# Attention's row maxima subtracted by TensorE, one exp for a step, and other places for loads and tiles

## The chip, the cores and the metric

One core of a Trainium2 chip runs the whole program in one launch. The metric is device time in microseconds (us). The engines are TensorE (PE, with its weight loads as PEld), VectorE (DVE), ScalarE (ACT), GpSimd (POOL) and SyncE (SP), which here only issues transfers.

## The reference, cut to what matters

```python
scores = scale * np.matmul(q, k.transpose(0, 1, 3, 2))        # (4, 8, 576, 64) inputs
...
scores = np.where(masks[None, :, :, :], scores, -1000000000.0)
scores = scores - np.max(scores, axis=-1, keepdims=True)
attn = np.exp(scores)
attn = attn / (np.sum(attn, axis=-1, keepdims=True) + 1e-09)
return np.matmul(attn, v).astype(np.float32)
```

Four heads see a plain window of 32 keys, four a dilated one (32 keys, 4 apart). The result, 2304 tokens by 512, goes through two mixtures of 8 experts. In the first, each token goes to one expert (288 tokens an expert) by a greedy assignment. In the second, every expert sees every token, and the outputs are weighed by a matrix P that 8 rounds of row and column scaling balance.

## The kernel before

**Attention.** The work is cut into 24 blocks (4 batches by 6 blocks of 96 queries), each against 128 keys. A unit holds kind 0 (plain) of one block and kind 1 (dilated) of the block after it, so there are 25 units (`NU`); the first and the last hold one kind alone. The loop over `n` (L303) gives the engines this order, and each engine works through its own instructions in it:

- `scores(n)`: PE writes the masks into two PSUM banks, as a bf16 identity (`idb`) times the mask table (L169), and adds q times k for eight heads (L176, f32, 64 rows each, so that two heads share the array).
- `row_max(n)`: DVE takes the maximum of each row and head (L182), and ACT turns it into a bias (L183).
- `p_trans(n-1)` on PE (L200), then `p_evac` of it, a copy of 768 columns from PSUM by DVE (L207).
- `exps(n)`: ACT, one instruction for each of the eight heads, the maximum as its bias (L192).
- `x_out(n-3)`: halves of the finished rows by ACT and POOL, stores by SP.
- `pv(n-2)`: PE multiplies by v (L218) and, in some iterations, adds the router's logits (L288) and turns finished rows (L258); DVE divides by the sums.

`scores` has two PSUM slots, `p_trans` and `pv` have one each. Beside this, `side` loads and splits the first weights of the second mixture (L742 on ACT, L744 on DVE). SP issues the loads: for the first batch, kind 1 of k and q with all 576 columns, then kind 0 of both, then v. ACT's queue issues the masks and an f32 identity, from which DVE makes `idb` (L293).

**Stage 1** (the router and the first mixture) ends with `m2_l1(8)` and `m2_l2(8)`. The first of these reads the tiles `x2` (L848, names x2h and x2l); the second reads the weights in the pool `m_w` (L936, names w1h and w1l). The balancing of P (`sinkhorn`, L1233) is placed between their matmuls by a planner (`interleave`).

**Stage 2** is the second mixture: seven experts over three blocks of 384 tokens, with products by a seven-multiplication scheme. `x_load` (L1048) brings a block's input into the tile `xb` with two transfers; `s_l1` (L1120) reads it. Pools opened in stage 2 lie one behind the other in the memory that stage 1 gave up: first `n_t` (29,184 bytes a partition by its tiles), then `n_x` with `xb` (21,504), then `n_h`. Stage 1's pools in that memory were, from low addresses to high, `m_x2` (36,864 bytes), then `m_w`.

Of the kernel before, what the change touches and what calls it, by code (L numbers as in the profile page):

```python
# [11 lines left out]
F32 = mybir.dt.float32  # L12
F16 = mybir.dt.float16
BF = mybir.dt.bfloat16
I32 = mybir.dt.int32
AF = mybir.ActivationFunctionType
OP = mybir.AluOpType
AX = mybir.AxisListType

B, H, S, D = 4, 8, 576, 64  # L20
# [3 lines left out]
QB = 96  # L24
# [7 lines left out]
SC = 0.125  # L32
# [26 lines left out]
MASK_ID, MASKS = attention_masks()  # L59
# [22 lines left out]
NU = len(UNITS)  # L82
# [29 lines left out]
def attention(tc, q, k, v, masks, wg, ident, xd, L, zero, side, early, keep, tables):  # L112

    nc = tc.nc
    with ExitStack() as ctx:
# [5 lines left out]

        raw, T, VR, SS, PP, PT, XT = {}, {}, {}, {}, {}, {}, {}
        src = {"q": q, "k": k}
        def load_qk(nm, b, kind):
            x = raw[nm, b, kind] = ld.tile([128, 2, S], F32, name="raw%s%d" % (nm, kind))
            nc.sync.dma_start(x, src[nm][b, :, 2 * kind:2 * kind + 2])

        def load_v(b, kind):
            x = VR[b, kind] = vp.tile([128, NJ, 4, D + 1], F32, name="rawv%d" % kind, bufs=2)
            nc.sync.dma_start(x, v[b, kind])  # L130

        def part(u, size):

            ks = list(UNITS[u])
            return slice(ks[0] * size // 2, (ks[-1] + 1) * size // 2)

        idf = one.tile([128, 128], F32)
        idb = one.tile([QB, QB], BF)
        idh = one.tile([QB, QB], F16)
        mk = one.tile([QB, MASKS.shape[1], 2, 128], BF)  # L140
        wgf = one.tile([128, 4, E], F32)
        wgh = one.tile([128, 4, E], F16)
        wgl = one.tile([128, 4, E], F16)
        for kind in (1, 0):
            for nm in "kq":
                load_qk(nm, 0, kind)
            if kind:
                nc.scalar.dma_start(mk, masks)
                nc.scalar.dma_start(idf, ident)
        load_v(0, 1)  # L150
        load_v(0, 0)

        def warm(n):
# [25 lines left out]
        def row_max(u):  # L179
            p, gs = SS[u], part(u, 4)  # L180
            nm = wk.tile([QB, 2, 4], F32, name="nm")
            nc.vector.tensor_reduce(nm[:, :, gs], p[:, :, gs], axis=AX.X, op=OP.max)  # L182
            nc.scalar.activation(nm[:, :, gs], nm[:, :, gs], AF.Copy, scale=-SC)  # L183
            PP[u] = nm

        def exps(u):
            p, nm, gs = SS.pop(u), PP[u], part(u, 4)
            e = wk.tile([QB, 2, 4, 128], F32, name="e")
            PP[u] = e
            for s in range(2):  # L190
                for g in range(gs.start, gs.stop):
                    nc.scalar.activation(e[:, s, g, :], p[:, s, g, :], AF.Exp, bias=nm[:, s, g:g + 1], scale=SC)  # L192
                yield

        def p_trans(u):
            e, gs = PP.pop(u), part(u, 4)
# [6 lines left out]
        def p_evac(u, p):  # L203
            gs = part(u, 4)
            t = PT[u] = wk.tile([128, 2, 4, QB], F32, name="pt")
            pp = p[:, :, :4 * QB].rearrange("p s (g q) -> p s g q", g=4)
            nc.vector.tensor_copy(t[:, :, gs], pp[:, :, gs])  # L207

        def pv(u, extra, turn=None):
            t = PT.pop(u)  # L210
# [79 lines left out]
            return lambda: nc.vector.tensor_copy(L[:, c, :], p)  # L290

        warm(18)
        nc.vector.tensor_copy(idb, idf[:QB, :QB])  # L293
        nc.vector.tensor_copy(idh, idf[:QB, :QB])
        loaded = []
        for kind in (1, 0):
            for nm in "kq":
# [2 lines left out]
            load_v(1, kind)  # L300
        xl = [one.tile([128, 2, 2, S], F16, name="xl%d" % kind) for kind in range(2)]
        first = S * (B - 1) // 128
        for n in range(NU + 2):  # L303
            if n < NU:
                scores(n)
                row_max(n)
            if 1 <= n <= NU:
                p_evac(n - 1, p_trans(n - 1))
            ex = exps(n) if n < NU else iter(())
            next(ex, None)  # L310
            if 3 <= n <= NU:
                x_out(n - 3)
            for _ in ex:
                pass
            if n == NU:
                early()
            if n in FILL:
                warm(FILL[n])
            if n >= 2:
                pv(n - 2, [loaded.pop(0)[1] for _ in range(1 if n < NU else 3) if loaded and loaded[0][0] <= n],  # L320
                   n - 3 if NU - 4 <= n <= NU else None)
            if n == 1:
                nc.gpsimd.dma_start(wgf, wg)
                tables()
            elif n == 4:
                nc.scalar.activation(wgh, wgf, AF.Copy, scale=SG)
                nc.vector.scalar_tensor_tensor(wgl, wgf, SG, wgh, op0=OP.mult, op1=OP.subtract)
            if 4 <= n:
                next(side, None)
            if n == 9:  # L330
                tables(True)
            b, c = divmod(n - NJ - 2, NJ)
            if 0 <= b < B - 2 and c < 2:
                load_v(b + 2, 1 - c)
            b, c = divmod(n - NJ, NJ)
            if 0 <= b < B - 2 and c < 2:
                for nm in "kq":
                    load_qk(nm, b + 2, 1 - c)
            b, c = divmod(n - 10, NJ)
            if 0 <= b < B - 1 and c < 3:  # L340
                c0, c1 = S * b // 128, S * (b + 1) // 128
                c0, c1 = c0 + 2 * c, min(c0 + 2 * c + 2, c1)
                if c1 > c0:
                    x_load(c0, c1)
                    loaded += [(n + 3, i) for i in range(c0, c1)]
            if n == NU - 1:
                x_load(first, first + 1)
            if n == NU:
                loaded += [(n, i) for i in (first, first + 1)]
# [36 lines left out]
THR = step_constants()  # L386
# [32 lines left out]
class Router:  # L419
# [35 lines left out]
    def tables(self, made):  # L455
        nc, col = self.nc, self.col
        tab, thr = self.source
        if not made:
            nc.gpsimd.dma_start(self.t, tab)
            nc.gpsimd.dma_start(self.thr, bass.AP(tensor=thr.tensor, offset=thr.offset, ap=[[0, 128], [1, THR.size]]))  # L460
            return
        nc.gpsimd.tensor_copy(self.tri, col("tri"))
        nc.gpsimd.tensor_copy(self.val, col("val").rearrange("p (c v) -> p c v", v=2))
        nc.gpsimd.tensor_copy(self.iota, col("iota"))
        nc.gpsimd.tensor_copy(self.diag, col("diag")[:E])
        nc.gpsimd.tensor_copy(self.group, col("group"))
# [200 lines left out]
class Moe:  # L667
# [34 lines left out]
    def tables(self, made):  # L702
        if made:
            self.nc.gpsimd.tensor_copy(self.id16, self.idf)
        else:
            self.nc.gpsimd.dma_start(self.idf, self.ident)

    def kept(self, ctx):
        self.xp = ctx.enter_context(self.tc.tile_pool(name="m_x", bufs=1, side="right"))
# [40 lines left out]
    def psum(self):  # L750
        return self.ps.tile([128, 512], F32, name="mm", bufs=6)

    def warm(self, n):

        p = self.psum()
        for _ in range(n):
            self.nc.tensor.matmul(p, self.zero[:, :128], self.zero, start=True, stop=True)

    def weights(self, key, fetch):

# [608 lines left out]
    def stage2(self, ctx):  # L1369


        pool = lambda n, b: ctx.enter_context(self.tc.tile_pool(name=n, bufs=b))
        self.tp, self.bp, self.hp = pool("n_t", 1), pool("n_x", 1), pool("n_h", 1)

        def part():
            lo = self.tp.tile([128, 2, 2, BLK], F32, name="r", bufs=2).bitcast(F16).rearrange(
                "p a b m -> p (a b m)")[:, :7 * 256].rearrange("p (k c) -> p k c", k=7)
            return self.tp.tile([128, 3, BLK], F32, name="S", bufs=1)[:, :, :256], lo

        def l1(e, n, b):  # L1380
            for j, ns in enumerate(self.s_l1(b)):
                if n and e + 1 < E and j in (0, 1, 3):
                    next(new)
                yield ns

        self.x_load(0)
        for _ in range(6):
            self.warm(1)
        for e in range(1, E):
            order = list(range(NB))[::1 if e % 2 else -1]  # L1390
            new = self.staged(e + 1, part) if e + 1 < E else iter(())
            for n, b in enumerate(order):
                if n == 0:
                    next(new, None)
                interleave(l1(e, n, b), self.side if (e, n) == (1, 0) else None)
                if n + 1 < NB:
                    self.x_load(order[n + 1])
                elif e + 1 < E:
                    self.last_piece()
                    self.w_load(0)  # L1400
                for j, _ in enumerate(self.s_l2(e)):
                    if j in (8, 10, 16, 20, 23, 43):
                        next(new, None)
                if n + 1 == NB:
                    for _ in new:
                        pass
                    if e + 1 < E:
                        self.w_load(1)
# [27 lines left out]


def constants():
    return dict(masks=MASKS.astype(ml_dtypes.bfloat16), ident=np.eye(128, dtype=np.float32), rtab=RTAB, thr=THR)


# [12 lines left out]
```

## Time and profile before

| what | value |
|---|---|
| time, median of 3 runs | 1805.51 us (1804.84 to 1808.44) |
| time of the profiled execution | 1803.2 us |
| its span, first to last instruction | 1801.4 us |
| PE busy | 1738.0 us (96%) |
| DVE busy | 1359.0 us (75%) |
| ACT busy | 852.7 us (47%) |
| mean granted TensorE clock | 0.982 |

A matmul's row in the trace begins when it begins to stream and ends when its last result is modelled to be written. Matmuls overlap, so what one costs in a row of many is the distance between starts, not its length. The granted clock is a share of 2.4 GHz. "x16" is a merged row of 16 instructions. The name behind an arrow in square brackets is what ended an idle time.

### The profile page before, as it was taken

Reading aid. Unit: us, or ns where it says so; the run is one execution under the profiler, and the core shown is the slowest. Engines: PE = TensorE matmul, PEld = TensorE weight load, DVE = VectorE, ACT = ScalarE, POOL = GpSimd, SP = SyncE. Lnnn points to the kernel's source line nnn. Section 1 sums busy time; section 2 is a strip of 40 time slices with the busy share of each in tenths; the row PEclk is TensorE's granted clock in tenths of the full one; section 3 lists DMA queues with packets and bytes.
Section 4 is the critical chain, followed back from the end, with each engine's and each line's share of the span. In section 5 each row is a group of like instructions: output and inputs, shape, how many; then the busy total and the mean of one; then the engine's idle time right before and its main releaser. Section 6 shows DMA issues by size and latency. Waiting matters only on the chain.

```text
span 1801.4 us, 35276 instructions
## 1 busy us (share of the span) xinstructions
PE 1738.0 (96%) x14464; PEld 1290.0 (72%) x14464; DVE 1359.0 (75%) x2583; ACT 852.7 (47%) x1581; POOL 239.6 (13%) x297
## 2 busy tenths in 40 slices
PE   9986899999999989999999999999999999999998
PEld 7864676667776657777777777777777777777776
DVE  6977785678744858878887888788788878887556
ACT  5853442343443345555554456444455544464433
POOL 2423331223320000000000000000000000000111
PEclk9977999999999999999999999999999999999999
DMA  8923441424442132445225443424452254433020
GB/s 295 288 65 108 121 121 61 131 78 121 143 139 67 57 130 98 170 154 201 114 89 206 159 150 133 162 101 170 157 197 116 90 202 159 150 134 154 36 97 36
DMA packets 105554, 241.20 MB, mean 134 GB/s; under 512 B 46192, under 2 KB 69888, under 8 KB 98480
## 3 DMA queue, kind: packets, MB, share of 16 engines
q1 hardware_dynamic: 84592, 151.27, 24.3%
q0 software_dynamic: 20544, 87.42, 13.8%
q8 instruction: 113, 1.85, 0.4%
q14 instruction: 49, 0.40, 0.1%
q10 hardware_dynamic: 256, 0.26, 0.0%
HBM read 173.63 MB, written 61.73 MB: 131 GB/s over the span
## 4 chain that ended last, share of the span: by engine, by line
PE 72%; DVE 11%; issue 10%; ACT 4%; DMA 2%; POOL 1%; SPq 0%; POOLq 0%; ACTq 0%; DVEq 0%
PE mm L1120 27%; PE mm L1158 23%; PE mm L848 8%; PE mm L936 5%; PE mm L892 2%; PE r L542 1%; PE ps_v L218 1%; DVE hl L1077 1%; PE ps_p L200 1%; PE ps_s L176 1%; POOL out_dram L1172 1%; DVE G L488 1%; DVE w1l L789 1%; DVE G L615 1%; ACT w1h L788 1%
## 5 line engine op out<-in xcount | busy, mean ns | idle before, releaser
L1120 PE MATMUL mm<-xb,w1h 128*128 128x384 f16 x2352 | 574.8, 327 | 7.8 <-issue 4.8
L1158 PE MATMUL mm<-w2h,hh 128*128 128x256 f16 x1764 | 480.8, 273 | 0.4
L1158 PE MATMUL mm<-w2h,hl 128*128 128x256 f16 x1764 | 480.8, 273 | 0.0
L1158 PE MATMUL mm<-w2l,hh 128*128 128x256 f16 x1764 | 480.8, 273 | 0.0
L1120 PE MATMUL mm<-xb,w1l 128*128 128x384 f16 x1176 | 383.9, 326 | 0.0
L1158 PEld LDWEIGHTS <-hh 128*128 128x128 f16 x3528 | 345.2, 98 | 43.1 <-issue 0.9
L1120 PEld LDWEIGHTS <-w1h 128*128 128x128 f16 x2352 | 230.3, 98 | 159.5 <-issue 11.4
L1158 PEld LDWEIGHTS <-hl 128*128 128x128 f16 x1764 | 172.6, 98 | 19.9
L1077 DVE TENSOR_TENSOR hl<-r,hh 128x1536 f16<-128x1536 f32 x84 | 147.5, 1756 | 42.7 <-ACT hh L1076 42.7
L1120 PEld LDWEIGHTS <-w1l 128*128 128x128 f16 x1176 | 115.2, 98 | 79.3 <-issue 3.5
L1072 ACT ACTIVATE r<-mm 128x384 f32<-128x384 f32 x252 | 119.1, 481 | 100.0 <-PE mm L1120 100.0
L1038 POOL DMA_DIRECT2D ws<-raw x48 | 26.1, 543 | 944.1 <-ACT raw L989 532.3
L1076 ACT ACTIVATE hh<-r 128x1536 f16<-128x1536 f32 x84 | 124.6, 1483 | 43.6 <-DVE r L1101 41.6
L1083 ACT ACTIVATE mm<-mm 128x384 f32<-128x384 f32 x84 | 40.3, 479 | 185.0 <-PE mm L1120 185.0
L1077 DVE TENSOR_TENSOR hl<-S,hh 128x1152 f16<-128x1152 f32 x84 | 113.6, 1352 | 0.0
L1168 DVE SCALAR_TENSOR_TENSOR acc<-t,P,acc 128x512 f32<-128x512 f32 x126 | 94.7, 752 | 4.5
L848 PE MATMUL mm<-xt,w1h 128*128 128x288 f16 x512 | 95.9, 286 | 1.7 <-DVE xt L865 1.7
L1076 ACT ACTIVATE hh<-S 128x1152 f16<-128x1152 f32 x84 | 96.3, 1147 | 0.0
L854 DVE SCALAR_TENSOR_TENSOR w1l<-mm,w1h 128x288 f16<-128x288 f32 (+1 forms) x120 | 50.3, 437 | 60.4 <-ACT w1h L853 59.8
L989 ACT ACTIVATE raw<-raw 128x1024 f16<-128x1024 f32 x48 | 50.6, 1055 | 87.3 <-DVE raw L973 45.5
L853 ACT ACTIVATE w1h<-mm 128x288 f16<-128x288 f32 (+1 forms) x120 | 46.9, 395 | 80.9 <-PE mm L848 78.4
L848 PE MATMUL mm<-x2l,w0h 128*128 128x256 f16 x288 | 79.9, 278 | 3.8 <-DVE x2l L897 3.8
(271 smaller groups left out, 2973.4 us busy)
## 6 DMA issues: line engine op xcount, KB each, us to landing
xb<-xw SPq DMA_DIRECT2D x30, 1344.0 KB, 8.7
ws<-raw POOLq DMA_DIRECT2D x48, 448.0 KB, 3.9
ws<-r POOLq DMA_DIRECT2D x48, 448.0 KB, 3.1
raw<-in_w2b_dram SPq DMA_DIRECT2D x32, 512.0 KB, 4.1
raw<-in_w1b_dram SPq DMA_DIRECT2D x56, 256.0 KB, 9.1
w1h<-ws SPq DMA_DIRECT2D x6, 1792.0 KB
w1l<-ws SPq DMA_DIRECT2D x6, 1792.0 KB
w2h<-ws SPq DMA_DIRECT2D x6, 1792.0 KB
```

What stands on the lines that cost most here:

```text
L848: nc.tensor.matmul(p, a[:, k, 128 * f:128 * (f + 1)], rhs(k, b), start=(done[f] == 1 and i == 0), stop=(done[f] == KT and i == 2), skip_gr ...
L853: nc.scalar.activation(h[0][:, f, :n], p, AF.Relu)
L854: nc.vector.scalar_tensor_tensor(h[1][:, f, :n], p, 0.0, h[0][:, f, :n], op0=OP.max, op1=OP.subtract)
L936: nc.tensor.matmul(p, a[:, f, c], b[:, f, :], start=(f == 0 and n == 0), stop=(f == FT - 1 and n == 2))
L989: self.nc.scalar.activation(hi[:, k], x, AF.Copy, scale=sw)
L1072: nc.scalar.activation(o, p, AF.Relu, scale=SH)
L1076: yield nc.scalar.activation(hq[0][:, i, k], x, AF.Copy)
L1077: yield V.tensor_sub(hq[1][:, i, k], x, hq[0][:, i, k])
L1083: nc.scalar.activation(Q[i], P[i], AF.Copy)
L1120: nc.tensor.matmul(p, w[u][:, 2 * j + i // 2, k, 128 * (i % 2):128 * (i % 2 + 1)], x[:, v, r, j], start=(q in (1, 5) and j == 0 and n == 0 ...
L1158: nc.tensor.matmul(p, h[u][:, i, a, 128 * t:128 * (t + 1)], w[v][:, i, b, :], start=(q in (1, 7) and i == 0 and j == 0), stop=(q in (2, 3) ...
L1168: V.scalar_tensor_tensor(self.acc[:, r, :], x, self.P[:, r, e:e + 1], self.acc[:, r, :], op0=OP.mult, op1=OP.add)
```

## The change

- `row_max` no longer makes a bias. A new step `less_max` lets PE subtract the maxima in PSUM: for each of the two banks, a matmul of minus the identity (`neg`, f32) with the maxima, repeated 128 times along each head.
- `exps` is one instruction for all heads of a unit. The copy of `p_evac` goes from DVE to ACT.
- The loop's order becomes `less_max(n)`, `exps(n)`, `scores(n+1)`, `row_max(n+1)`, `p_trans(n-1)`, and so on; `scores(0)` and `row_max(0)` stand ahead of it.
- The first batch's q and k come in two runs of columns (192, then 384). The bf16 identity comes in one transfer with the masks.
- Tables for the router (wg, rtab, thr, ident) are loaded by SP's queue, not POOL's.
- In stage 2 the pool of `xb` is opened ahead of `n_t`. Six filling matmuls of 512 columns become two of 1 column and one of 512.

```diff
-            nc.scalar.activation(nm[:, :, gs], nm[:, :, gs], AF.Copy, scale=-SC)
             PP[u] = nm
 
+        def less_max(u):
+            p, nm, gs = SS[u], PP[u], part(u, 4)
+            for s in range(2):
+                nc.tensor.matmul(p[:, s, gs, :], neg, nm[:, s, gs].unsqueeze(2).to_broadcast([QB, gs.stop - gs.start, 128]),
+                                 start=False, stop=True, skip_group_check=True)
+
         def exps(u):
-            p, nm, gs = SS.pop(u), PP[u], part(u, 4)
-            e = wk.tile([QB, 2, 4, 128], F32, name="e")
-            PP[u] = e
-            for s in range(2):
-                for g in range(gs.start, gs.stop):
-                    nc.scalar.activation(e[:, s, g, :], p[:, s, g, :], AF.Exp, bias=nm[:, s, g:g + 1], scale=SC)
-                yield
+            p, gs = SS.pop(u), part(u, 4)
+            e = PP[u] = wk.tile([QB, 2, 4, 128], F32, name="e")
+            nc.scalar.activation(e[:, :, gs], p[:, :, gs], AF.Exp, scale=SC)
...
-            nc.vector.tensor_copy(t[:, :, gs], pp[:, :, gs])
+            nc.scalar.activation(t[:, :, gs], pp[:, :, gs], AF.Copy)
...
-        nc.vector.tensor_copy(idb, idf[:QB, :QB])
-        nc.vector.tensor_copy(idh, idf[:QB, :QB])
+        nc.vector.tensor_scalar(neg, idf[:QB, :QB], -1.0, None, op0=OP.mult)
...
+        scores(0)
+        row_max(0)
         for n in range(NU + 2):
             if n < NU:
-                scores(n)
-                row_max(n)
+                less_max(n)
+                exps(n)
+            if n + 1 < NU:
+                scores(n + 1)
+                row_max(n + 1)
             if 1 <= n <= NU:
                 p_evac(n - 1, p_trans(n - 1))
-            ex = exps(n) if n < NU else iter(())
-            next(ex, None)
             if 3 <= n <= NU:
                 x_out(n - 3)
-            for _ in ex:
-                pass
...
+        nc.scalar.dma_start(mki, masks)
         for kind in (1, 0):
             for nm in "kq":
-                load_qk(nm, 0, kind)
+                load_qk(nm, 0, kind, slice(0, 2 * QB))
             if kind:
-                nc.scalar.dma_start(mk, masks)
                 nc.scalar.dma_start(idf, ident)
-        load_v(0, 1)
+                load_v(0, 1)
+        for kind in (1, 0):
+            for nm in "kq":
+                load_qk(nm, 0, kind, slice(2 * QB, S))
         load_v(0, 0)
...
-                nc.gpsimd.dma_start(wgf, wg)
+                nc.sync.dma_start(wgf, wg)
...
-        self.tp, self.bp, self.hp = pool("n_t", 1), pool("n_x", 1), pool("n_h", 1)
+        self.bp, self.tp, self.hp = pool("n_x", 1), pool("n_t", 1), pool("n_h", 1)
...
         self.x_load(0)
-        for _ in range(6):
-            self.warm(1)
+        for n in 1, 1, 512:
+            self.warm(1, n)
```

## Rows read from the trace of the kernel before

**Rows 1.** Busy time by stretch: PE, PEld, DVE, ACT, POOL; granted clock, DMA share, GB/s
```profile
18.10:103.70 85.60, 84.75 (x1046) 74.73 (x1045) 77.71 (x131) 69.21 (x230) 33.97 (x30) 1.00 0.81 246
...
628.70:641.70 13.00, 5.60 (x22) 2.64 (x20) 3.10 (x13) 1.07 (x2) 0.00 (x0) 0.74 0.67 252
...
641.70:1801.00 1159.30, 1153.04 (x8809) 861.52 (x8807) 909.28 (x1401) 571.75 (x911) 71.23 (x132) 1.00 0.36 136
```

**Rows 2.** Timeline of PE, iterations 3 and 4: start us, length us, line, operation
```profile
18.15 0.60 PE L169 MATMUL ps_s<-mk,idb 96*96 96x256 bf16 x4
...
21.78 0.60 PE L169 MATMUL ps_s<-mk,idb 96*96 96x256 bf16 x4
...
23.36 0.88 PE L200 MATMUL ps_p<-idf,e 96*128 96x96 f32 x8
24.08 1.50 PE L218 MATMUL ps_v<-rawv,pt 128*96 128x65 f32 x16
25.41 0.60 PE L169 MATMUL ps_s<-mk,idb 96*96 96x256 bf16 x4
```

**Rows 3.** Timeline of PE: the logits of n=13; the starts of n=24 and n=25
```profile
60.09 0.17 PE L288 MATMUL ps_v<-wgh,xT 128*128 128x8 f16 x1
...
60.39 0.62 PE L169 MATMUL ps_s<-mk,idb 96*96 96x256 bf16 x4
...
103.68 0.38 PE L169 MATMUL ps_s<-mk,idb 96*96 96x256 bf16 x2
...
108.70 0.33 PE L200 MATMUL ps_p<-idf,e 96*128 96x96 f32 x2
```

**Rows 4.** Groups by line and shape, 18.1 to 103.7: busy us, mean ns
```profile
L192 ACT ACTIVATE e<-ps_s,nm 96x128 f32<-96x128 f32 x166 | 46.8, 367 | 0.7
...
L182 DVE TENSOR_REDUCE nm<-ps_s 96x8 f32<-96x1024 f32 x21 | 25.5, 1214 | 1.4 <-PE ps_s L176 1.4
```

**Rows 5.** The page's costliest groups: an ACT conversion of 1024 columns
```profile
L989 ACT ACTIVATE raw<-raw 128x1024 f16<-128x1024 f32 x48 | 50.6, 1055 | 87.3 <-DVE raw L973 45.5
```

**Rows 6.** Two lines' matmuls (ns least/median/most), and a pair of them in the timeline
```profile
L1265 PE MATMUL r<-P,mean x16: 286/286/444, 591.8 to 639.7; 128*128 128x144 f32 x16
...
L848 PE MATMUL mm<-xt,w1h x512: 282/286/297, 160.7 to 564.2; 128*128 128x288 f16 x171
...
613.88 0.41 PE L1265 MATMUL r<-P,mean 128*128 128x144 f32 x2
```

**Rows 7.** Timeline of the first 13 us
```profile
1.20 6.72 PE L156 MATMUL ps_v<-zero 128*128 128x512 f16 x18 [1.20 <-DVE zero L445]
...
8.10 0.21 DVE L293 CAST idb<-idf 96x96 bf16<-96x96 f32 x1 [6.66 <-DMA idf<-in_ident_dram]
...
12.51 1.12 PE L176 MATMUL ps_s<-rawk,rawq 64*96 64x128 f32 x16 [1.71 <-DMA rawq<-in_q_dram]
```

**Rows 8.** Timeline around the start of stage 2, all engines and SP's queue
```profile
584.52 19.76 SPq L962 DMA_DIRECT2D raw<-in_w2b_dram  x4
...
614.68 0.27 PE L848 MATMUL mm<-x2l,w0h 128*128 128x256 f16 x1
...
628.33 0.38 PE L936 MATMUL mm<-w1h,xg 128*128 128x512 f16 x1
...
628.74 0.82 SPq L1051 DMA_DIRECT2D xb<-xw  x2
...
630.51 0.31 DVE L1262 TENSOR_TENSOR P<-P,rs 128x144 f32<-128x144 f32 x1
...
637.88 0.48 PE L1120 MATMUL mm<-xb,w1h 128*128 128x384 f16 x1 [2.56 <-DMA xb<-xw]
...
641.67 0.49 PE L1120 MATMUL mm<-xb,w1h 128*128 128x384 f16 x2
...
642.00 0.33 PE L1120 MATMUL mm<-xb,w1l 128*128 128x384 f16 x1
```

**Rows 9.** SP's loads of xb: issue to landing, us
```profile
DMA to landing us min/median/max: 8.6/8.7/10.0
```

More of the change, by code (lines that the diff above doesn't have):

```diff
@@ L123, in attention, with load_qk @@
         src = {"q": q, "k": k}
-        def load_qk(nm, b, kind):
-            x = raw[nm, b, kind] = ld.tile([128, 2, S], F32, name="raw%s%d" % (nm, kind))
-            nc.sync.dma_start(x, src[nm][b, :, 2 * kind:2 * kind + 2])
+        def load_qk(nm, b, kind, c=slice(0, S)):
+            if (nm, b, kind) not in raw:
+                raw[nm, b, kind] = ld.tile([128, 2, S], F32, name="raw%s%d" % (nm, kind))
+            nc.sync.dma_start(raw[nm, b, kind][:, :, c], src[nm][b, :, 2 * kind:2 * kind + 2, c])
         def load_v(b, kind):
@@ L137, in attention @@
         idf = one.tile([128, 128], F32)
-        idb = one.tile([QB, QB], BF)
-        idh = one.tile([QB, QB], F16)
-        mk = one.tile([QB, MASKS.shape[1], 2, 128], BF)
+        neg = one.tile([QB, QB], F32, name="neg")
+        nm_ = MASKS[0].size
+        mki = one.tile([QB, nm_ + QB], BF, name="mk")
+        mk = mki[:, :nm_].rearrange("p (t k c) -> p t k c", k=2, c=128)
+        idb = mki[:, nm_:]
         wgf = one.tile([128, 4, E], F32)
@@ L458, in tables @@
         if not made:
-            nc.gpsimd.dma_start(self.t, tab)
-            nc.gpsimd.dma_start(self.thr, bass.AP(tensor=thr.tensor, offset=thr.offset, ap=[[0, 128], [1, THR.size]]))
+            nc.sync.dma_start(self.t, tab)
+            nc.sync.dma_start(self.thr, bass.AP(tensor=thr.tensor, offset=thr.offset, ap=[[0, 128], [1, THR.size]]))
             return
@@ L705, in tables @@
         else:
-            self.nc.gpsimd.dma_start(self.idf, self.ident)
+            self.nc.sync.dma_start(self.idf, self.ident)
     def kept(self, ctx):
@@ L751, in psum, with warm @@
         return self.ps.tile([128, 512], F32, name="mm", bufs=6)
-    def warm(self, n):
-        p = self.psum()
+    def warm(self, n, width=512):
+        p = self.psum()[:, :width]
         for _ in range(n):
-            self.nc.tensor.matmul(p, self.zero[:, :128], self.zero, start=True, stop=True)
+            self.nc.tensor.matmul(p, self.zero[:, :128], self.zero[:, :width], start=True, stop=True)
     def weights(self, key, fetch):
@@ L1438, in constants @@
 def constants():
-    return dict(masks=MASKS.astype(ml_dtypes.bfloat16), ident=np.eye(128, dtype=np.float32), rtab=RTAB, thr=THR)
+    return dict(masks=np.concatenate([MASKS.reshape(QB, -1), np.eye(QB)], 1).astype(ml_dtypes.bfloat16), ident=np.eye(128, dtype=np.float32), rtab=RTAB, thr=THR)
 def kernel(q, k, v, moe_w_gate, moe_w1, moe_w2, moe2_w_gate, moe2_w1, moe2_w2):
```

## The prediction

> **What bounds the kernel now.** I began with the table of stretches [rows 1]. In the loop of attention, 18.1 to 103.7 us, PE is busy 84.75 of 85.60 us at the full clock (2.4 GHz), DVE 77.71, ACT 69.21. Since a busy PE need not be at its peak, I then read the starts. Iteration 4 runs from 21.78 to 25.41, 3.63 us, with no idle time on PE [rows 2]: masks and scores 1.58, transposes 0.72, the product with v 1.33. So PE's stream sets the pace there. Iteration 3 starts at 18.15 [rows 2] and iteration 24 at 103.68 [rows 3], 85.53 us for 21 iterations. PE's own work in them is 21 x 3.63 = 76.2, nine groups of logits at 0.30 (60.09 to 60.39, rows 3) = 2.7, and turned rows, ten transposes at 0.09 (0.72 over 8, rows 2) = 0.9, together 79.8. The other 5.7 us are small waits, for ACT's exps or for DVE; lighter engines beside PE can give back at most that.
>
> The second place is the start of stage 2 [rows 8]. The last matmul of stage 1 starts at 628.33. SP issues the two loads of `xb` at 628.74, although its queue had nothing more to issue after 584.52 + 19.76 = 604.28. It waited for the memory. The second load lands for PE at 637.88. The clock of the stretch is 0.74 of full, part of it at 1.2 GHz, and PE works 5.60 of 13.00 us [rows 1]. From 641.70 to the end PE is busy 1153.04 of 1159.30 us [rows 1], so an earlier start there comes out at the end, and so does a later end of attention, after which the router works in a chain on the finished logits.
>
> **What `less_max` costs on PE.** The trace has no matmul of 512 f32 columns. It has f32 products of 144 columns, sixteen records for the eight matmuls of `sinkhorn` (eight rounds), thus two records a matmul. One lasts 286 ns, as long as an f16 record of 288 columns, and two in a row take 0.41 us, so the second starts 0.41 - 0.286 = 0.124 us after the first [rows 6]. An f32 column thus passes at half the pace of an f16 one, twice. A record of 512 columns should hold PE for 0.124 x 512/144 = 0.44 us, a matmul 0.88, the two matmuls of a full unit 1.76 us. I take 1.75; the 23 full and 2 half units make 24 x 1.75 = 42 us. Bounds: below, one f16-paced pass for each record, half of it, 0.88 a unit; above, 1.95, if about 0.2 us is lost at each change of operand (an estimate: twice the 0.09 of a transpose).
>
> The Trainium skill ("TensorE: Matmul & The Clock Gate", section "Back-to-back issue gap") gives a warm matmul N/2.4 + 2.5 ns, with no word on f32, which makes 0.86 us of the four records. The pair of f32 records [rows 6] runs at half that pace, so I go by the row; by the page the sum below would end some 21 us lower.
>
> **What leaves PE's way.** Eight exps of 0.28 apart (46.8 us over 166, rows 4) and the small bias copy leave ACT; one exp of 1024 columns enters, about 1.05 like a conversion of that width [rows 5], and the copy of 768 columns, 3/4 of that, 0.8. ACT's step shrinks by about 0.6 us and lies far below the new PE step. DVE loses that copy. Both are hidden behind PE then, and would cost nothing unless they exceed 3.63 + 1.75 = 5.38 us. The maxima take 1.21 us [rows 4]. `less_max(n+1)` waits for them, and everything behind it on PE's queue waits too, but the transposes and the product with v, 2.05 us, stand in between [rows 2]. If that cover were gone, some 0.3 us more with signal times, 1.5 an iteration would show. The stalls of 5.7 us go.
>
> **The loop, summed.** Iterations 3 to 23 after: 21 x 5.38 = 113.0, logits 2.7, turned rows 0.9, iteration 24 with half a `less_max` 0.88 + 0.72 + 1.33 + 0.33 (its turned rows) = 3.3: 119.9 us. Before, from 18.15 to 108.70, where iteration 25 begins [rows 2, 3]: 90.55. Difference +29.3.
>
> **The beginning.** The warm matmuls end at 1.20 + 6.72 = 7.92 [rows 7]. Before, `idb` came at 8.10 + 0.21, and unit 1 waited for kind 0 of q until 12.51. The smaller loads end both, but `scores(0)` still stands behind the warm matmuls. After, I reckon: scores(0) to 8.6; maxima of a half unit with signals to 9.6; half a `less_max` to 10.5; scores(1) 1.6, to 12.1; maxima and signals 1.5, to 13.6 (four fillers inside); `less_max(1)` to 15.35; scores(2) to 16.95; maxima to 18.45; `less_max(2)` to 20.2; scores(3), transposes of unit 1 and half a product, 3.0, to 23.2, where iteration 3 begins. Before: 18.15. Difference +5.0 (bounds +3 and +8, if the maxima hide fully in other work, or one load, 3 us, comes late). The second run of columns is first needed by scores(2), about 15; the whole loads had landed by 12.51. The router's tables, moved to SP, stand there behind loads that wait for nothing and are first used in iterations 4 and 9: no cost. If SP were held, their users would wait, ACT and POOL first. The end of attention keeps its order: 0 (bounds -1 and +1). Attention: **+34.3 us**.
>
> **Stage 2's tile.** With `n_x` first, `xb` lies over `x2` and the gap below it, not over `m_w`, by the sizes of the tiles. The last matmul on `x2` starts at 614.68 [rows 8]; the loads can go at about 615, and land in 8.7 to 10.0 [rows 9], by 625, before PE needs them at about 628.55, when the last matmul has passed. Three us of cover remain; a load later than that costs what it is late. Then the fillers, 0.3; six products at 0.165 (two of them from 641.67 to 642.00, rows 8) to 629.8; the planner's product on P waits for DVE's 630.51 + 0.31 [rows 8] and ends the pause at about 631.3; seven more products end at 632.4. In the trace the fourteenth product starts at 641.67. Gain **-9.3** (bounds -10.5, if the pause is hidden, and -3, if the clock falls in it and the loads are late). The fillers' removal is inside this sum.
>
> **The rivals.**
> 1. *The f32 records run at the f16 pace.* Then a unit costs 0.88, 24 x 0.87 = 20.9 us less: 1809.7. For it speaks only that no row has 512 columns; against it, rows 6. The page named above would have it so. 0.07.
> 2. *The other side: `less_max` is nearly free, as a single f16-paced pass,* 0.44 a unit. Then attention grows by 34.3 - 24 x 1.31 = 2.9, stage 2 gives 9.3: 1799.1, faster. It decides below 1.75 - 25.0/24 = 0.71 us a unit. Two records a matmul speak against it. 0.05.
> 3. *The move of `xb` does nothing,* because the loads wait for another tile at the same address or for a weight buffer on SP's queue: 1830.5 + 9.3 = 1839.8. The queue stands empty from 604.28, which speaks against it. 0.10.
> 4. *A new wait each iteration:* DVE's maxima come late for `less_max`, some 0.3 us x 21 = 6: 1836.8. The 2.05 us of cover speak against it; that DVE also converts weights in every second iteration, ahead of the next maxima, for it. 0.08.
>
> **How the numbers follow.** 34.3 - 9.3 = +25.0 us. The profiled execution took 1803.2 with a span of 1801.4, so it would become 1828.2. It lies 2.3 under the median of the runs, so I forecast 1805.5 + 25.0 = 1830.5 for the median. This case has 0.67, with its own range of 1825 to 1836 (beginning +/-3, records +/-2); 0.03 is left for anything else. From 1822 to 1841 lie this case and rivals 3 and 4, 0.85 together; rivals 1 and 2 lie outside. A change within 0.2% (3.6 us) is about what this measurement can't tell from none. Faster by more: rival 2 and a little of the rest, 0.06; within: 0.03; slower: 0.91.
>
> **What would show it.** In the changed profile, four records of 512 f32 columns a unit, 0.43 to 0.44 us between starts, and mask-to-mask starts 5.4 us apart in iterations 4 to 12. One exp near 1.05 us. The router's first labels some 34 us later. The loads of `xb` issued some 13 us before the last matmul of stage 1, PE's pause at the start of stage 2 below 2 us, and the clock there full. I would be wrong if the records start 0.22 us apart or less, if PE idles before `less_max`, or if SP still issues `xb` after the last product of stage 1.

## The result and the profile after

Over four runs of each on one chip the changed kernel takes 1829.57 us (1826.35 to 1830.67) and the kernel before 1806.97: a ratio of 1.0125, with a 95% interval of 1.0104 to 1.0145. It is slower by 22.6 us, between 18.8 and 26.2 by the interval; the forecast was +25.0. The profiled execution took 1830.67 us, with a span of 1828.9, 27.5 more than the span before.

In the order of time, the profiled executions part like this:

| point in the trace | before, us | after, us | later by |
|---|---|---|---|
| iteration 3 begins | 18.15 | 22.52 | 4.4 |
| iteration 25 begins | 108.70 | 142.81 | 34.1 |
| last logits of attention | 121.0 | 154.94 | 33.9 |
| last product that reads `x2` | 614.68 | 649.96 | 35.3 |
| last matmul of stage 1 | 628.33 | 665.00 | 36.7 |
| last product of stage 2 | 1795.27 | 1822.63 | 27.4 |

So nearly all of the loss arises in attention, 2.8 us are added on the way through the router and stage 1, and stage 2 gives 9.3 back.

The changed loop first. The timeline of PE over one iteration and the start of the next (start, length, line, operation), which answers to [rows 2]:

```profile
27.95 1.91 PE L194 MATMUL ps_s<-nm,neg 96*96 96x512 f32 x4
29.70 0.60 PE L175 MATMUL ps_s<-mk 96*96 96x256 bf16 x4
30.23 1.12 PE L182 MATMUL ps_s<-rawk,rawq 64*96 64x128 f32 x16
31.27 0.88 PE L207 MATMUL ps_p<-idf,e 96*128 96x96 f32 x8
31.99 1.50 PE L225 MATMUL ps_v<-rawv,pt 128*96 128x65 f32 x16
33.32 1.05 PE L194 MATMUL ps_s<-nm,neg 96*96 96x512 f32 x2
```

L194 is `less_max`. Its two matmuls stand as four records and hold PE from 27.95 to 29.70, 1.75 us, 0.4375 a record. What follows is the old iteration, with its old lengths: 3.62 us to the next `less_max`. No row has idle time before it, so one iteration is 5.37 us here, and 5.38 in the mean of the next ones.

The same loop by groups of line and shape (busy us, mean ns; then idle time of the engine before them and its releaser), answering to [rows 4, 5]:

```profile
L194 PE MATMUL ps_s<-nm,neg 96*96 96x512 f32 x80 | 38.3, 601 | 0.0
...
L188 DVE TENSOR_REDUCE nm<-ps_s 96x8 f32<-96x1024 f32 x19 | 23.2, 1221 | 29.4 <-PE ps_s L182 29.4
...
L200 ACT ACTIVATE e<-ps_s 96x1024 f32<-96x1024 f32 x20 | 20.5, 1024 | 25.8 <-issue 25.8
...
L214 ACT ACTIVATE pt<-ps_p 128x768 f32<-128x768 f32 x19 | 15.4, 811 | 23.5 <-PE ps_p L207 23.5
```

The one exp takes 1024 ns and the copy 811 ns. What matters is the right-hand column: DVE stood idle 29.4 us for scores, ACT 23.5 us for transposes, and PE not at all before `less_max`. Eight exps became one on an engine that didn't set the pace, and the time that ACT gained became idle time.

Busy time by stretch (PE, PEld, DVE, ACT, POOL; granted clock, DMA share, GB/s): the loop, the end of stage 1, the first 13 us of stage 2, against [rows 1]:

```profile
27.90:135.00 107.10, 107.10 (x1021) 78.65 (x1020) 54.51 (x104) 53.97 (x78) 24.72 (x27) 1.00 0.62 171
...
657.60:661.00 3.40, 3.40 (x9) 1.04 (x8) 3.19 (x11) 2.08 (x3) 0.00 (x0) 0.50 0.67 248
665.20:678.20 13.00, 12.42 (x78) 7.42 (x77) 6.51 (x19) 5.60 (x10) 0.00 (x0) 1.00 0.01 1
```

PE is busy 107.10 of 107.10 us in the loop. The second row, 3.4 us at the 1.2 GHz level, is taken up again below. At the start of stage 2 it is busy 12.42 of 13.00 at the full clock, where before it was busy 5.60 at 0.74.

That start in the timeline of SP's queue, against [rows 8]:

```profile
633.12 6.45 SPq L969 DMA_DIRECT2D raw<-in_w2b_dram  x2
650.27 0.82 SPq L1058 DMA_DIRECT2D xb<-xw  x2
```

And in the timeline of PE:

```profile
657.04 0.48 PE L1272 MATMUL r<-P,mean 128*128 128x144 f32 x2 [1.89 <-DVE P L1269]
...
665.00 0.38 PE L943 MATMUL mm<-w1h,xg 128*128 128x512 f16 x1
665.21 0.43 PE L764 MATMUL mm<-zero 128*128 128x1 f16 x3
665.48 0.49 PE L1127 MATMUL mm<-xb,w1h 128*128 128x384 f16 x2
...
667.19 0.48 PE L1272 MATMUL r<-P,mean 128*128 128x144 f32 x2 [0.58 <-DVE P L1269]
667.51 0.49 PE L1127 MATMUL mm<-xb,w1h 128*128 128x384 f16 x2
```

The loads of `xb` leave 0.3 us after the last product on `x2` begins and 14.7 us before the last matmul of stage 1. The first product of stage 2 then follows that matmul by 0.48 us. What is left of the pause is 0.58 us for the planner's P.

The beginning, in PE's timeline, against [rows 7]:

```profile
1.20 6.25 PE L162 MATMUL ps_v<-zero 128*128 128x512 f16 x18 [1.20 <-DVE zero L452]
7.29 0.38 PE L175 MATMUL ps_s<-mk 96*96 96x256 bf16 x2
...
9.07 1.11 PE L194 MATMUL ps_s<-nm,neg 96*96 96x256 f32 x4 [0.79 <-DVE nm L188]
...
10.55 1.12 PE L182 MATMUL ps_s<-rawk,rawq 64*96 64x128 f32 x16
...
12.99 1.96 PE L194 MATMUL ps_s<-nm,neg 96*96 96x512 f32 x4 [0.35 <-DVE nm L188]
...
17.75 1.96 PE L194 MATMUL ps_s<-nm,neg 96*96 96x512 f32 x4 [0.84 <-DVE nm L188]
...
22.52 1.96 PE L194 MATMUL ps_s<-nm,neg 96*96 96x512 f32 x4
```

PE doesn't wait for q here: unit 1's scores begin at 10.55 instead of 12.51. But `less_max` waits for maxima three times (0.79, 0.35 and 0.84 us; these waits stood in the prediction's sum, and from iteration 3 on there is none), and each full unit carries its 1.75 us, so iteration 3 begins later all the same.

### The profile page after: what moved, and what is told of

It is laid out like the page before. It is cut to its first block, busy times and chain, and to the rows that moved or that the text cites. A ratio compares the mean times of both kernels' runs of the same rounds, so it can differ in the third digit from the quotient of the medians.

```text
span 1828.9 us, 35255 instructions
## 1 busy us (share of the span) xinstructions
PE 1777.1 (97%) x14561; PEld 1306.1 (71%) x14561; DVE 1335.7 (73%) x2557; ACT 840.0 (46%) x1414; POOL 228.8 (13%) x293
## 3 DMA queue, kind: packets, MB, share of 16 engines
q0 software_dynamic: 20384, 87.05, 13.6%
## 4 chain that ended last, share of the span: by engine, by line
PE 62%; issue 9%; DVE 5%; ACT 2%; DMA 1%; POOL 1%; POOLq 0%; SPq 0%; ACTq 0%; DVEq 0%
PE mm L1127 27%; PE mm L1165 23%; PE mm L855 5%; PE mm L943 4%; PE mm L899 2%; DMA raw<-in_w1b_dram 1%; POOL out_dram L1179 1%; DVE hl L1084 1%; ACT raw L996 1%; PE r L549 0%; DMA raw<-in_w2a_dram,widx 0%; DVE w1l L796 0%; PE mm L870 0%; DVE w1l L999 0%; DVE G L495 0%
```

## The experiments

My theory: the price is PE's time for f32 records, 1.75 us a full unit, and everything else in attention hides behind PE; in stage 2 the place of `xb` is worth some 9 us. The rival for attention was that the new order of the loop costs by its waits, with or without the subtraction. The experiments ran on two further chips, where the kernel before took 1822.1 us (bf16 maxima, no subtraction, subtraction twice, stage 2's part) and 1815.2 (the other four). Every ratio is to the kernel before on the same chip.

**The maxima in bf16.** From the changed kernel, both operands of the subtraction become bf16. What is taken off a row is then its maximum rounded, which stands in the row's sum just as in its exps and falls out of their quotient.

```diff
-        neg = one.tile([QB, QB], F32, name="neg")
+        neg = one.tile([QB, QB], BF, name="neg")
...
-            nm = wk.tile([QB, 2, 4], F32, name="nm")
+            nm = wk.tile([QB, 2, 4], BF, name="nm")
```

> The changed kernel with minus the identity and the maxima in bf16 instead of f32 (every score of a row and head still has the same number taken off, now a maximum rounded to bf16). Theory, PE's stream sets the pace and the f32 records cost what they occupy: one record a matmul instead of two, each 512 columns at f16's pace, so 2 x 0.215 = 0.43 us a unit instead of 1.75; 24 x 1.32 = 31.7 us less than the changed kernel, about 1798 us, 8 us below the kernel before; iterations 4 to 12 at 4.06 us. Rival, the loss comes from the new chain (scores, maxima on DVE, subtraction, exp): the chain is as long as it was, and the time stays within 5 us of the changed kernel's 1829.6.

Measured: 1814.53 us, ratio 0.9959 (0.9944 to 0.9974). PE's timeline:

```profile
27.71 0.60 PE L194 MATMUL ps_s<-nm,neg 96*96 96x512 bf16 x2
28.15 0.60 PE L175 MATMUL ps_s<-mk 96*96 96x256 bf16 x4
...
31.77 0.60 PE L194 MATMUL ps_s<-nm,neg 96*96 96x512 bf16 x2
```

One record a matmul in place of two, and 0.44 us for the unit in place of 1.75. The step is 4.06 us and the last logits come at 124.03, 30.9 us earlier than in the changed kernel; 24 units at 1.31 make 31.4. The order, the number of matmuls and their columns are as before, so the type of the operands alone takes nearly the whole loss away. The gain over the kernel before that is left is stage 2's: the last logits still come 3.0 us later than the 121.0 of before, and stage 2 takes 1157.67 us, as in the changed kernel (1157.63).

**No subtraction.** From the changed kernel:

```diff
             if n < NU:
-                less_max(n)
                 exps(n)
```

> The changed kernel with the subtraction of the maxima left out (the maxima are still computed and nobody uses them). Theory: the whole of 24 x 1.75 = 42 us goes, iterations 4 to 12 at 3.63 us, about 1788 us. Rival, other engines were about to become the bound (ACT with exp, copy and conversions at 3.1 us, DVE): then PE waits and less than 36 us go.

Measured: 1807.95 us, ratio 0.9929 (0.9903 to 0.9955): 12.9 us less than the kernel before by the ratio, 14.2 by the medians. PE's timeline:

```profile
29.91 0.60 PE L175 MATMUL ps_s<-mk 96*96 96x256 bf16 x4
...
33.54 0.60 PE L175 MATMUL ps_s<-mk 96*96 96x256 bf16 x4
```

PE's waits of that run from 27 to 110 us (engine, tile and line, who ended them; us in total, times, longest):

```profile
PE ps_v L225 <- ACT x L241: 2.4, 3, 1.2
PE ps_v L295 <- DMA xT<-xd: 1.5, 1, 1.5
PE ps_p L207 <- ACT pt L214: 0.2, 1, 0.2
```

The step falls to 3.63, that of iteration 4 before [rows 2], so the new order costs nothing by itself in the loop. The last logits come at 117.19, 37.75 us earlier than in the changed kernel and not 42. Of the 4 us that are missing, 2.5 are waits in the late iterations: they sum to 4.1 us here, where the changed kernel has only 1.6, all on ACT's `x`. Some 0.8 us more are lost ahead of iteration 4, where unit 1 waits 2.12 us for q, until 10.54, and PE runs at a granted clock of 0.50 from 11.7 to 15.0 us. The last 0.9 us was not traced. So the expectation's rival, that other engines come near to being the bound, is right in a small part, for the last iterations. The trace puts what goes at 37.75 us, above the 36 that was set as the mark; the times can't tell, as the two ratios, taken on different chips, differ by some 35 us.

**The subtraction twice.** From the changed kernel, the call stands two times.

```diff
                 less_max(n)
+                less_max(n)
                 exps(n)
```

> The changed kernel with the subtraction issued twice for each unit (the maxima are taken off twice). Theory: 24 x 1.75 = 42 us more, about 1872 us, iterations 4 to 12 at 7.1 us. Rival, part of the first subtraction's price was waiting for the maxima on DVE: then the second, which waits for nothing, costs clearly less than the first, under 35 us.

Measured: 1887.70 us, ratio 1.0361 (1.0337 to 1.0385), 65.6 over the kernel before. PE's timeline:

```profile
41.16 3.63 PE L194 MATMUL ps_s<-nm,neg 96*96 96x512 f32 x8
44.63 0.60 PE L175 MATMUL ps_s<-mk 96*96 96x256 bf16 x4
...
48.26 1.91 PE L194 MATMUL ps_s<-nm,neg 96*96 96x512 f32 x4
```

Eight records hold PE for 3.47 us, the step is 7.10, the last logits come at 195.31, 40.4 later than in the changed kernel, so the first subtraction's price was not a wait for the maxima (the rival's mark was 35). With the runs above that is a line: 0, 0.44, 1.75 and 3.47 us on PE a unit against steps of 3.63, 4.06, 5.38 and 7.10. What is put on PE comes out in full.

**The copy of pt back on DVE.** From the run with bf16 maxima:

```diff
-            nc.scalar.activation(t[:, :, gs], pp[:, :, gs], AF.Copy)
+            nc.vector.tensor_copy(t[:, :, gs], pp[:, :, gs])
```

> The changed kernel with minus the identity and the maxima in bf16, and the copy of the transposes (768 columns) on DVE again. Theory, PE's stream sets the pace and the copy is hidden on either engine: steps of 4.06 us in iterations 4 to 12, the time within 2 us of the bf16 kernel with the copy on ACT (0.996 of the kernel before). Rival, DVE's maxima come late behind the copy: steps over 4.2 us, 4 us or more slower than that kernel.

Measured: 1808.06 us, ratio 0.9963 (0.9947 to 0.9978), beside 0.9959 with the copy on ACT, on the other chip. In the groups by line and shape the copy has moved and takes 944 ns:

```profile
L214 DVE COPY pt<-ps_p 128x768 f32<-128x768 f32 x18 | 17.0, 944 | 0.0
```

The step is 4.06 in both. The copy is hidden on either engine, even at this shorter step.

**Whole loads of q and k.** From the changed kernel, the first batch comes in one load each again; the identity stays beside the masks and the tables on SP.

```diff
-                load_qk(nm, 0, kind, slice(0, 2 * QB))
+                load_qk(nm, 0, kind)
...
-                load_v(0, 1)
-        for kind in (1, 0):
-            for nm in "kq":
-                load_qk(nm, 0, kind, slice(2 * QB, S))
+        load_v(0, 1)
```

> The changed kernel with the first batch's q and k loaded whole again (all 576 columns at once; the identity still comes with the masks). Theory: kind 0 of q is late again, near 12.4 us, unit 1's scores end 2 us later, and each later iteration begins 2 us later, with the same step of 5.38 us: iteration 3 at about 24.5 in place of 22.5, 25 us over the kernel before. Rival, the maxima and the subtraction set the start anyway: iteration 3 within 0.5 us of 22.5.

Measured: 1839.56 us, ratio 1.0135 (1.0115 to 1.0154). PE's timeline:

```profile
1.20 5.47 PE L159 MATMUL ps_v<-zero 128*128 128x512 f16 x18 [1.20 <-DVE zero L449]
...
7.14 0.68 PE L179 MATMUL ps_s<-rawk,rawq 64*96 64x128 f32 x8 [0.25 <-DMA rawq<-in_q_dram]
...
10.08 1.12 PE L179 MATMUL ps_s<-rawk,rawq 64*96 64x128 f32 x16
...
22.06 1.96 PE L191 MATMUL ps_s<-nm,neg 96*96 96x512 f32 x4
```

My theory of the beginning falls here. I had expected iteration 3 some 2 us later; it begins at 22.06, before the changed kernel's 22.52, because the warm matmuls ended sooner in this execution (6.67 instead of 7.45). That the time lies 24.3 us over the kernel before, with 25 expected, is no support for the theory: the ratio's interval overlaps the changed kernel's. The whole loads cost one wait of 0.25 us. Nor did they hold q back: unit 1's scores run at 10.08 without a wait, so its q had landed by then, 2 us sooner than in the kernel before, where PE waited for it until 12.51 (12.3 in the two runs below that keep its loop and its loads). With the loads in two runs PE waited for the same q until 10.54 (no subtraction), 10.33 (bf16 with the copy on DVE) and 10.11 (the last run below). So the two runs of columns did not bring q forward; something else in the change did. What is left are the tables, four transfers that POOL issued between 1.29 and 3.10 us in the kernel before, and the identity beside the masks; no run has either alone.

**Stage 2's part alone.** From the kernel before:

```diff
-        self.tp, self.bp, self.hp = pool("n_t", 1), pool("n_x", 1), pool("n_h", 1)
+        self.bp, self.tp, self.hp = pool("n_x", 1), pool("n_t", 1), pool("n_h", 1)
...
-        for _ in range(6):
-            self.warm(1)
+        for n in 1, 1, 512:
+            self.warm(1, n)
```

> The kernel before with the changes to stage 2 alone (pool of xb first, fillers of 1, 1 and 512 columns). Theory: the loads of xb go at about 615 us in place of 628.7, and 9 to 10 us are gained, about 1797 us. Rival, the gain seen in the changed kernel comes with attention's later end (less traffic at that time) or from chance in the clock: 0 to -4 us.

Measured: 1813.54 us, ratio 0.9963 (0.9948 to 0.9978), 6.7 us less by the ratio (4.0 to 9.5 by its interval), 8.6 by the medians. SP's queue and PE in the timeline:

```profile
628.19 0.82 SPq L1051 DMA_DIRECT2D xb<-xw  x2
...
641.51 0.38 PE L936 MATMUL mm<-w1h,xg 128*128 128x512 f16 x1
...
641.99 0.49 PE L1120 MATMUL mm<-xb,w1h 128*128 128x384 f16 x2
...
644.15 0.48 PE L1265 MATMUL r<-P,mean 128*128 128x144 f32 x2 [1.01 <-DVE P L1262]
```

The loads leave 13.3 us before stage 1's last matmul, products follow it at once, and stage 2 takes 1158.96 us from that matmul to its last product, 8.0 less than the 1166.94 of before.

**The fillers alone.** The same without the move of `n_x`.

```diff
-        for _ in range(6):
-            self.warm(1)
+        for n in 1, 1, 512:
+            self.warm(1, n)
```

> The kernel before with stage 2's fillers alone changed (1, 1 and 512 columns in place of six of 512), the pool of xb where it was. Theory: the loads of xb still go after the last product of stage 1 and land some 9 us later, so nothing is gained: 0 to +2 us, the clock at the start of stage 2 as low as before. Rival, the fillers were in the way: -1 us or better, and then part of the gain with both changes is theirs.

Measured: 1817.70 us, ratio 1.0009 (0.9991 to 1.0027). SP's queue and PE:

```profile
642.00 0.38 PE L936 MATMUL mm<-w1h,xg 128*128 128x512 f16 x1
...
642.41 0.82 SPq L1051 DMA_DIRECT2D xb<-xw  x2
...
648.46 0.48 PE L1120 MATMUL mm<-xb,w1h 128*128 128x384 f16 x1 [5.82 <-issue]
651.50 0.48 PE L1120 MATMUL mm<-xb,w1h 128*128 128x384 f16 x1 [2.56 <-DMA xb<-xw]
```

The loads are issued after the last matmul again, and PE stands still. Stage 2 takes 1166.84 us, as in the kernel before (1166.94), where the three other runs on this chip, all with the tile moved, have 1157.05 to 1157.17: 9.7 us less on one chip. So the gain belongs to the tile's place, and the fillers by themselves have no part that can be measured. The move with the old fillers was not run: with the loads early, six fillers at 0.22 us would hold PE about 1 us longer than the 0.27 of the new ones (an estimate from the rows), and how much of that the wait for P would hide is open.

**The old loop with the other parts.** Stage 2's part and the loads, the identity and the tables' queue as changed, with the kernel before's attention loop: to the run of stage 2's part this was added (cut):

```diff
+        nc.scalar.dma_start(mki, masks)
         for kind in (1, 0):
             for nm in "kq":
-                load_qk(nm, 0, kind)
+                load_qk(nm, 0, kind, slice(0, 2 * QB))
...
-        nc.vector.tensor_copy(idb, idf[:QB, :QB])
-        nc.vector.tensor_copy(idh, idf[:QB, :QB])
...
-                nc.gpsimd.dma_start(wgf, wg)
+                nc.sync.dma_start(wgf, wg)
```

> The kernel before with the changes to stage 2, the loads in two runs, the identity beside the masks and the tables on SP's queue, and attention's loop as it was (eight exps with a bias, no subtraction on PE). Theory: stage 2 gives 9 us; the two-run loads let unit 0 begin behind the warm matmuls at about 7.5 and unit 1 at about 9, where q kept it until 12.5: 3 us more, 0.993 of the kernel before, below both kernels. Rival, ACT's exps of the first units (2.2 us each) take back what the loads give: 0.996, no better than stage 2 alone.

Measured: 1805.85 us, ratio 0.9934 (0.9917 to 0.9952): 9.4 us faster than the kernel before by the medians, 12.0 by the ratio. PE's timeline of the beginning:

```profile
10.11 1.12 PE L181 MATMUL ps_s<-rawk,rawq 64*96 64x128 f32 x16 [1.11 <-DMA rawq<-in_q_dram]
...
15.75 0.60 PE L174 MATMUL ps_s<-mk 96*96 96x256 bf16 x4
```

The table of stretches of that run, for the end of attention:

```profile
105.00:124.00 19.00, 16.02 (x186) 14.31 (x185) 11.29 (x33) 8.78 (x26) 5.67 (x7) 0.54 0.50 93
```

Without `less_max` the beginning does gain: iteration 3 begins at 15.75, 2.2 us earlier than the 17.95 of the run with stage 2's part alone. Unit 1, expected at about 9, still waits 1.11 us for q, until 10.11. By the run with whole loads, this gain isn't owed to the two runs of columns. In this execution the end of attention ran at a granted clock of 0.54, mostly the 1.2 GHz level (0.75 in the kernel before, from 103.7 to 121.0), and its last logits came at 123.69, later than the 121.0 of before; so this 2.2 us is shown at iteration 3 and not at the end of attention. The version beats both kernels; that it beats stage 2's part alone (0.9963) is likely but not clear, as the intervals overlap and the chips differ.

## Why the prediction held

**The bound.** That PE's stream sets the pace of attention held, by the line of four prices above and by rows that keep their length: in iterations 3 to 23 of the changed kernel the eight transposes take 0.72 us each time, to 0.01. The busy share alone, 107.10 of 107.10 us, would not show it. The kernel before was busy 84.75 of 85.60 us too, and yet 5.7 us lay beyond PE's own work, as the prediction reckoned. They hide in rows like these, of iteration 18 before:

```profile
78.53 0.72 PE L200 MATMUL ps_p<-idf,e 96*128 96x96 f32 x4
79.72 1.06 PE L200 MATMUL ps_p<-idf,e 96*128 96x96 f32 x4 [0.47 <-ACT e L192]
```

The eight transposes take 2.1 us here, to the product with v at 80.63. The last ones start 0.26 us apart, behind the single exps, and each is 0.25 to 0.30 us long, so nearly all of the waiting looks busy. Over iterations 3 to 23 the transposes exceed 0.72 us by 5.3 us in sum. With one exp they don't, and those stalls went, as predicted.

**The f32 record.** Predicted 0.44 us, measured 0.4375. The step from two records of 144 columns [rows 6] to four of 512 columns carried over by columns alone. The pace of the f16 records [rows 6], taken for the f32 ones, was rival 1; four records 0.4375 apart and a forecast of 1809.7 against 1829.6 rule it out, and rival 2, below it, with it.

The Trainium skill ("TensorE: Matmul & The Clock Gate", section "Back-to-back issue gap") gives N/2.4 + 2.5 ns as the warm gap of a single matmul, 216 ns for 512 columns. The run with bf16 maxima agrees, with 0.22 us for each of its two matmuls; the f32 matmul took 0.875, four times that, and the measurement decides.

**What was costed at nothing.** The exp of 1024 columns (predicted 1.05, measured 1.02), the copy (0.8 and 0.81) and the maxima (1.22) lie behind PE, and rival 4's wait doesn't appear in the loop. The swap of the copy between engines, without effect, shows that cover also at 4.06 us a step.

**The sums.** From iteration 3 to 25 predicted 119.9 us, measured 142.81 - 22.52 = 120.3; so +29.7 for +29.3. The beginning +4.4 for +5.0, inside its bounds, as the warm matmuls ended 0.5 us sooner than I took from before (7.45 against 7.92). One reading in it was wrong without harm to the sum: that the smaller loads end the wait for q. It ended with whole loads as well, and with small ones PE still waited 1.1 to 2.1 us in three runs where unit 1 asked for q earlier than here. The end of attention -0.2 for 0. Attention: +33.9 for +34.3.

**Between the stages** I had put nothing, and 2.8 us stand there in the profiled execution. Half of it, 1.4, lies between the last product on `x2` and the last matmul, 15.04 us against 13.65: after its wait of 1.89 us for P, PE ran its records at double spacing, at a granted clock of 0.50, to 661.0. That is not the change's: the run of the fillers alone, in which only what comes after this stretch differs from the kernel before, shows it too, at a clock of 0.89 and 14.95 us. Of the ten profiled executions seven have it (14.9 to 15.1 us), and three, of the kernel before, with bf16 maxima and with stage 2 alone, run at 1.00 in 13.6, all after the same wait of 1.9 us. What decides it was not found. The other 1.3 us lie between the last logits and the last product on `x2`, 495.02 us against 493.68. They were not traced to one place; on each of the other two chips the same stretch differs between executions, by 3.9 and 5.5 us, so it may be chance.

**Stage 2.** Predicted -9.3, measured 1157.63 - 1166.94 = -9.3. The order was as reckoned: loads early, fillers, six products, the product on P, then the stream; the pause was 0.58 us. That the tenth agrees is luck. The thirteenth product on `xb` starts 3.49 us after the last matmul, where it started 13.34 after it before: 9.85 less, as P came 0.5 us sooner than reckoned, and 0.5 us is lost again later in stage 2. (The product at 641.67, which the prediction takes for the fourteenth, is the thirteenth; that moves its sum by 0.1.) Rival 3 (the move does nothing) is out, and the runs with and without the move of `n_x` give that cause on the chip: 13.3 us ahead of the last matmul in the one, 0.4 us behind its start in the other.

In sum the profiled span gives 33.9 + 2.8 - 9.3 = +27.4, and the medians +22.6, with the forecast of +25.0 inside the interval of the latter. The two differ because the profiled execution of the changed kernel is the longest of its four runs, and that of the kernel before, 1803.2 us, is shorter than all of its four. So the terms are checked to some tenths by the trace, and their sum by the times only to about 4 us.

One reason for the change fell with the runs, though not a step of the sum: the smaller loads are worth next to nothing, one wait of 0.25 us in the changed kernel. What does bring iteration 3 forward once `less_max` is out of the stream is, by elimination, the tables on SP's queue or the identity beside the masks; that was argued and not run alone.

## What to carry to other kernels

Moving work from an engine with slack to the one that sets the pace costs its full length, however many instructions it saves elsewhere: read the idle column before counting instructions, and the spacing of the rows where an engine looks busy throughout. On PE, ask for the operand type first: where the number taken off cancels later, as a softmax's maximum does, bf16 operands did the same subtraction in a quarter of the time; even so, attention only came near to where it had been. When a stage starts with a stall, look at what its first tile lies on; putting `xb` over a tile whose last reader starts 13 us earlier was worth 8 to 10 us in the profiles (6.7 by the ratio of its own run, between 4.0 and 9.5) and cost nothing that was seen, and one bundle of edits held that gain beside a loss more than three times its size.

## What the runs showed that was not expected

The same 18 warm matmuls took 6.72, 6.25 and 5.47 us in three executions, and the first mask moved with them, from 7.29 to 6.51 in the last two; that is more than the two runs of columns did in the changed loop. Their starts lie 0.43 us apart at first and 0.22 later, and the pace doubled at 6.3 us in the kernel before, 5.4 in the changed one and 4.1 with whole loads. The same wait of 1.9 us for P was followed by 3.4 us at the 1.2 GHz level in seven executions and not in three, 1.4 us apart.

And the kernel before took 1807.0, 1822.1 and 1815.2 us on three chips, a spread of 0.8%, larger than most of the differences that were looked for; only ratios within one chip tell them apart. In the profiles most of the spread lies in one place, from the last logits to the last product on `x2`, the router and most of stage 1: 493.7 and 495.0 us on the first chip, 507.2 to 512.7 on the second, 500.3 to 504.2 on the third. Stage 2 has no part in it: with the tile moved it takes 1157.05 to 1158.96 us on all three; with the tile in its old place, 1166.94 and 1166.84 on two. What makes the router's stretch longer on one chip than on another was not looked for.
